# A decode kernel bound by its cache reads: part of the query weights on eight DMA engines, smaller work after the last load

## Chip, cores, metric

One core of one Trainium2 chip. The metric is the device time of one execution in microseconds (us), median over executions.

## The reference

One token (1 x 448) goes through attention with a cache of 65,536 positions for 8 key/value heads of 256, and through a token mixer; a gate mixes the two results.

```python
x = A_x                                             # [1, 1, 448]
g = sigmoid((x * gate_w).sum(-1, keepdims=True))
q = (x @ wq).reshape(1, 1, 16, 256)                 # wq [448, 4096]
p = softmax(q @ k_cache.T / 16)                     # k, v: [1, 8, 65536, 256]
a = (p @ v_cache).reshape(1, 1, 4096) @ wo          # wo [4096, 448]
u = gelu(layernorm(x).T * w1 + b1)
b = (u @ w2 + b2).T
out = g * a + (1 - g) * b
```

Keys and values are 537 MB of the 544 MB that the kernel reads.

## The kernel before

Forty-eight K blocks and as many V blocks (5 or 6 MB each) are loaded in turn into two K buffers and one V buffer. One queue (SP) issues nearly everything. The query weights use the V buffer first. Their first 384 rows lie three to a partition; the other 64 rows are cut in two halves of 2048 columns, which makes 128 rows.

```python
TAIL = 4
...
wqa = vbuf[:, 0:KA * HQ * DH].rearrange("p (k n) -> p k n", k=KA)
wqb = vbuf[:, KA * HQ * DH:KA * HQ * DH + 8 * DH]
do.dma("sp", vbuf[:, 0:KA * HQ * DH], A_wq[0:DA, :].rearrange("(p k) n -> p (k n)", k=KA), writes=["wqa"])
do.dma("sp", wqb, A_wq[DA:D, :].rearrange("r (hh n) -> (r hh) n", hh=2), writes=["wqb"])
...
load_k(0)
load_k(1)
```

The last V block comes in four pieces. The first two go through matmuls with V as the moving operand (`upright`), the last two through small ones with V as the stationary operand (`turned`). `TAIL` is the number of 128-row groups in the last piece. Two pieces of output weights follow.

```python
edges = [0, nlast - TURN - SB, nlast - TURN, nlast - TAIL, nlast]   # 0, 40, 56, 76, 80
...
dve.wait_ge(s_fp, 2)
drain_pv(False).then_inc(s_fd, 1)
dve.tensor_scalar(out=row[:], in0=acc[0:1, 0:D], scalar1=bias[:, 0:1], scalar2=None, op0=ALU.add).then_inc(s_fd, 1)
pe.wait_ge(s_fd, 1)
o_turn(2)
pe.wait_ge(s_last[2], 16)
turned(edges[2], edges[3])
pe.wait_ge(s_last[3], 16)
turned(edges[3], edges[4]).then_inc(s_fp, 1)
dve.wait_ge(s_fp, 3)
heads().then_inc(s_fd, 1)
pe.wait_ge(s_fd, 2)
for a in range(4):                       # bias sums into the output's accumulator
    pe.matmul(acc4[...], lhsT=one_f[:, 0:1], rhs=row[...], start=True, stop=False, ...)
pe.wait_ge(s_fd, 3)
for k in range(4):                       # output projection
    r, cc = divmod(k, 2)
    if cc == 0:
        pe.wait_ge(s_wl[r], 16)
    ...
```

The softmax here doesn't subtract the row's maximum and nothing guards it: scores larger than these inputs give would overflow.

Of the kernel before, what the change touches and what calls it, by code (L numbers as in the profile page):

```python
# [9 lines left out]
BF16 = mybir.dt.bfloat16  # L10
ACT = mybir.ActivationFunctionType
ALU = mybir.AluOpType
# [3 lines left out]
HKV = 8  # L16
# [12 lines left out]


TURN = 24
TAIL = 4

GELU_C0 = 0.7978845608028654
GELU_C1 = 0.044715
# [59 lines left out]
def kernel(  # L95
# [16 lines left out]
    D = A_x.shape[-1]  # L112
# [3 lines left out]
    KA = D // 128  # L116
    DA = KA * 128
    DR = D - DA
    DQ = D // 4
# [7 lines left out]
    const = ctx.enter_context(tc.tile_pool(name="const", bufs=1))  # L127
# [8 lines left out]
    misc = psum.tile([128, 512], FP32, name="misc")  # L136
    den_ps = psum.tile([128, 512], FP32, name="den_ps")
    acc = psum.tile([128, 512], FP32, name="acc")
    acc4 = psum.tile([128, 512], FP32, name="acc4")

    x_row = const.tile([1, D], BF16, name="x_row")
# [10 lines left out]
    one_f = const.tile([1, 128], FP32, name="one_f")  # L152
    col_f = const.tile([128, 1], FP32, name="col_f")
    zero_b = const.tile([1, D], BF16, name="zero_b")
    xd = const.tile([1, 2, 128], BF16, name="xd")
    xw = const.tile([128, KA + 2, 128 + HKV - 1], BF16, name="xw")
    xg = const.tile([1, D], FP32, name="xg")
    gate = const.tile([128, 2], FP32, name="gate")
    half_g = const.tile([128, 1], FP32, name="half_g")
    bias = const.tile([1, 1], FP32, name="bias")  # L160
# [26 lines left out]
    row = const.tile([1, D], FP32, name="row")  # L187
# [19 lines left out]
    def critical():  # L207
        do = Order(nc)
        pe, dve, act, pool, sp = nc.tensor, nc.vector, nc.scalar, nc.gpsimd, nc.sync
# [19 lines left out]

        wqa = vbuf[:, 0:KA * HQ * DH].rearrange("p (k n) -> p k n", k=KA)  # L230
        wqb = vbuf[:, KA * HQ * DH:KA * HQ * DH + 8 * DH]
        do.dma(
            "sp", vbuf[:, 0:KA * HQ * DH], A_wq[0:DA, :].rearrange("(p k) n -> p (k n)", k=KA),
            writes=["wqa"],
        )
        do.dma("sp", wqb, A_wq[DA:D, :].rearrange("r (hh n) -> (r hh) n", hh=2), writes=["wqb"])

        def load_k(i):
            n = steps[i] * SB * DH
# [24 lines left out]
        for k, src in enumerate((B_w1[0, :], B_b1, B_w2[:, 0])):  # L264
# [7 lines left out]
                out=ident[:], in_=ident[:], compare_op=ALU.not_equal, fill=1.0, base=0,  # L272
# [23 lines left out]
        for hh in range(2):  # L296
            do(
                "dve", lambda e: e.tensor_copy(
                    out=xd[:, hh, :].rearrange("o (r two) -> o r two", two=2)[:, :, hh],
                    in_=x_row[:, DA:D],  # L300
                ), reads=["x_row"], writes=["xd"],
            )
        x_ps = misc[:, 480:480 + KA + 2]

        def turn_x(e):
            for k in range(KA + 2):
                if k < KA:
                    src = x_row[:, 0:DA].rearrange("o (p k) -> o p k", k=KA)[:, :, k]
                else:
                    src = xd[:, k - KA, :]  # L310
                last = e.matmul(
                    x_ps[:, k:k + 1], lhsT=src, rhs=one_b[0:1, 0:1], start=(k == 0),
                    stop=(k == KA + 1), skip_group_check=True,
                )
            return last

# [1 line left out]
        do(  # L318
            "dve", lambda e: e.tensor_copy(
                out=xw[:, :, HKV - 1:HKV + 96:32],  # L320
                in_=x_ps.rearrange("p (k o) -> p k o", o=1).to_broadcast([128, KA + 2, 4]),
            ), reads=["x_ps"], writes=["xw"],
        )

# [3 lines left out]
            reads=["x_row", "gw_row"], writes=["xg"],  # L328
# [3 lines left out]
            reads=["xg"], writes=["zb"],  # L332
# [3 lines left out]
            writes=["zb1"],  # L336
# [4 lines left out]
            reads=["one_f", "zb", "zb1"], writes=["z_ps"],  # L341
        )
        for col, sign in ((0, -1.0), (1, 1.0)):
            do(
                "act", lambda e: e.activation(
                    out=gate[:, col:col + 1], in_=z_ps[:, 0:1], func=ACT.Exp, scale=sign
# [5 lines left out]
                out=gate[:], in0=gate[:], scalar1=1.0, scalar2=None, op0=ALU.add  # L352
# [5 lines left out]
                out=half_g[:], in0=gate[:, 1:2], scalar1=0.5, scalar2=None, op0=ALU.mult  # L358
# [4 lines left out]
                out=bias[:], in0=z_ps[0:1, 1:2], in1=gate[0:1, 1:2], op=ALU.mult  # L363
# [6 lines left out]
            reads=["one_b", "x_row"], writes=["xb_ps"],  # L370
# [5 lines left out]
                out=veps[:], in0=mv[:, 1:2], scalar1=1e-5, scalar2=None, op0=ALU.add  # L376
# [4 lines left out]
            reads=["veps", "mhalf"], writes=["rstd"],  # L381
        )
        for _ in range(2):
            do(
                "dve", lambda e: e.tensor_tensor(out=nt[:], in0=rstd[:], in1=rstd[:], op=ALU.mult),
                reads=["rstd"], writes=["nt"],
# [3 lines left out]
                reads=["nt", "veps"], writes=["nt"],  # L390
# [3 lines left out]
                    out=nt[:], in0=nt[:], scalar1=-0.5, scalar2=1.5, op0=ALU.mult, op1=ALU.add  # L394
# [4 lines left out]
                reads=["rstd", "nt"], writes=["rstd"],  # L399
# [3 lines left out]
                out=h_bc[:], in0=xb_ps, scalar1=mv[:, 0:1], scalar2=rstd[:, 0:1],  # L403
                op0=ALU.subtract, op1=ALU.mult,
# [17 lines left out]
        for k, (t, key) in enumerate(((w1T, "w1T"), (b1T, "b1T"))):  # L422
            do(
                "dve", lambda e: e.tensor_copy(out=t[:], in_=w_ps[:, k * NF:(k + 1) * NF]),
                reads=["w_ps"], writes=[key],
# [3 lines left out]
                out=hw2[:], in0=w_ps[:, 2 * NF:3 * NF], scalar1=half_g[:, 0:1], scalar2=None,  # L429
                op0=ALU.mult,  # L430
# [6 lines left out]
                out=mask[:].rearrange("p m x -> p (m x)"), in_=pat[:].rearrange("p m x -> p (m x)")  # L437
# [4 lines left out]
        q_ps = sc  # L442

        def project(e):
            for n in range(HKV):
                half, at = divmod(n, 4)
                for k in range(KA + 1):
                    if k < KA:
                        rhs = wqa[:, k, n * 512:(n + 1) * 512]
                    else:  # L450
                        k, rhs = KA + half, wqb[:, at * 512:(at + 1) * 512]
                    last = e.matmul(
                        q_ps[:], lhsT=xw[:, k, HKV - 1 - n:HKV - 1 - n + 128], rhs=rhs,
                        start=(n == 0 and k == 0), stop=(n == HKV - 1 and k >= KA),
                        skip_group_check=True,
                    )
            return last

        do("pe", project, reads=["wqa", "wqb", "xw"], writes=["q_ps"])
        do.need("sp", writes=["wqa", "wqb"])  # L460
        load_v(0)
        load_wo(0)
        do(
# [1 line left out]
                out=q_row[:].rearrange("p (m c y) -> p m y c", c=2, y=32),  # L465
                in_=q_ps[:].rearrange("p (m y c) -> p m y c", c=2, y=32),
# [4 lines left out]
                out=qr[:].rearrange("p r q n -> p (r q n)"), in_=q_row[:]  # L471
# [11 lines left out]
        for r in range(2):  # L483
# [4 lines left out]
                skip_group_check=True,  # L488
# [21 lines left out]
        for r in range(2):  # L510
            at = (HKV - 1) * 512 + r * DH
            sp.dma_start(
                out=wo[:, r, :, :].rearrange("p c n -> p (c n)"),
                in_=A_wo[at:at + DH, :].rearrange("(p c) n -> p (c n)", c=2),
# [52 lines left out]
        with nc.Fori(0, HKV, 1, engines=[DVE], head_slot={DVE: 128}) as turn_v:  # L567
            for c in range(PER):
# [21 lines left out]
                else:  # L590
# [6 lines left out]
                        out=og[:], in0=og[:], scalar1=dsum[:, 0:1], scalar2=None, op0=ALU.add  # L597
# [8 lines left out]
        for i in range(total):  # L606
            g, c = divmod(i, PER)
            ins = act.activation(  # L608
                out=p_t[:], in_=sc[:], func=ACT.Exp, scale=scale, accum_out=den[:, c:c + 1]
# [3 lines left out]
            b, ph = divmod(i - 2, 2)  # L613
            if not 0 <= b < NF:
                continue
            if ph == 0:
                ins = act.activation(  # L617
                    out=t_b[:], in_=h_bc[:], func=ACT.Square, scale=w1T[:, b:b + 1],
                    bias=b1T[:, b:b + 1],
# [9 lines left out]
        for b in range(NF):  # L629
            work = [  # L630
                lambda: pool.tensor_scalar(  # L631
                    out=u_b[:], in0=h_bc[:], scalar1=w1T[:, b:b + 1], scalar2=b1T[:, b:b + 1],
                    op0=ALU.mult, op1=ALU.add,
# [48 lines left out]
        def o_turn(width):  # L682
            for half, m in enumerate((L0, H0)):
                for cc in range(2):
                    ins = pe.matmul(  # L685
                        o_ps[:, cc, 0:width if half == 0 else 2],
                        lhsT=og[:, half * DH + cc:(half + 1) * DH:2],
                        rhs=mask[:, m:m + (width if half == 0 else 2), 0],
                        start=(half == 0 and cc == 0), stop=(half == 1 and cc == 1),
                        skip_group_check=True,  # L690
                    )
            return ins
# [54 lines left out]
        def turned(lo, hi):  # L747
# [10 lines left out]
        pe.wait_ge(s_mp, 6 * NF)  # L758
        pe.matmul(
            acc[0:1, 0:D], lhsT=col_f[:], rhs=ymix[:], start=False, stop=True, skip_group_check=True,  # L760
        )
        take(pe, s_pt)
        pe.wait_ge(s_last[0], 16)
        upright(edges[0], edges[1])
# [2 lines left out]
            den_ps[:, 0:2], lhsT=dsum[:].to_broadcast([128, 128]), rhs=mask[:, D0:D0 + 2, 0],  # L767
            start=True, stop=True,
        ).then_inc(s_fp, 1)
        dve.wait_ge(s_fp, 1)  # L770
        rden_gate(den_ps[:, 0:2])
        pe.wait_ge(s_last[1], 16)
        upright(edges[1], edges[2]).then_inc(s_fp, 1)
        dve.wait_ge(s_fp, 2)
        drain_pv(False).then_inc(s_fd, 1)
        dve.tensor_scalar(
            out=row[:], in0=acc[0:1, 0:D], scalar1=bias[:, 0:1], scalar2=None, op0=ALU.add
        ).then_inc(s_fd, 1)
        pe.wait_ge(s_fd, 1)
        o_turn(2)  # L780
        pe.wait_ge(s_last[2], 16)
        turned(edges[2], edges[3])
        pe.wait_ge(s_last[3], 16)
        turned(edges[3], edges[4]).then_inc(s_fp, 1)
        dve.wait_ge(s_fp, 3)
        heads().then_inc(s_fd, 1)
        pe.wait_ge(s_fd, 2)
        for a in range(4):
            pe.matmul(  # L789
                acc4[32 * a:32 * a + 1, 0:DQ], lhsT=one_f[:, 0:1], rhs=row[:, DQ * a:DQ * (a + 1)],  # L790
                start=True, stop=False, tile_position=(0, 32 * a), skip_group_check=True,
            )
        pe.wait_ge(s_fd, 3)
        for k in range(4):
            r, cc = divmod(k, 2)
# [6 lines left out]
                    tile_position=(0, 32 * a), skip_group_check=True,  # L802
                )
        ins.then_inc(s_fp, 1)
        dve.wait_ge(s_fp, 4)
        dve.tensor_copy(out=res[0:97, :], in_=acc4[0:97, 0:DQ]).then_inc(s_fd, 1)  # L806
        s_out = nc.alloc_semaphore("s_out")
        sp.wait_ge(s_fd, 4)
# [37 lines left out]
```

## Time and profile before

| | before |
|---|---|
| median of 3 runs | 1265.99 us (1265.82 to 1266.15) |
| span of the profiled run | 1264.1 us |
| DMA queue 1 | 99.7% of sixteen engines' time |
| last V piece lands, last of sixteen engines | 1259.20 us |
| last output weights land | 1260.41 us |
| output projection ends | 1261.01 us |

The DMA engines are the bound: queue 1 takes 99.7% of their time, and no compute engine is busy for over 57%. What decides tenths of a microsecond is when the latest of the sixteen engines lands its last bytes, and how much work follows. Both are read from the chain of waits and from the trace's record of semaphore increments, sixteen for each full load. An engine ends its share of a load with a closing record, a packet of 4 bytes; the increment that the waiting engine sees follows it (in the last query-weight load: closing records from 11.14 to 12.21 us, increments from 11.46 to 12.52, 0.30 to 0.37 us later, paired in order of time). A load has landed at its last increment. "Narrow load" below means the load that runs on eight engines alone, "low" are those eight and "high" the other eight. The end of the projection is the end of its last matmul's record (1261.01); the chain puts it at 1261.04. The prediction below shows the lines.

### The profile page before, as it was taken

The page shows a single profiled execution, that of the slowest core. Times are in us where ns is not written, and L with a number is a line of the kernel's source. Part 1 is how long each engine was busy: PE and PEld are TensorE (multiplying, and loading weights), DVE is VectorE, ACT ScalarE, POOL GpSimd, SP SyncE. Part 2 cuts the span into 40 slices and gives each one's busy share as a digit, 9 for nine tenths or more (in the row PEclk, how much of TensorE's full clock was granted, in tenths as well). Part 3 has the DMA queues.
Part 4 walks back from the last instruction along what each step waited for, and adds up shares of the span by engine and source line. Part 5 has one row for each costly group of instructions (what it writes and reads, how often), then busy time and mean ns, then how long its engine had stood idle before and what let it go on. Part 6 is the DMA issues. An engine that isn't in the chain of part 4 may idle for free. (4 is left out here: it accounts for less than half of the span.)

```text
span 1264.1 us, 10623 instructions
## 1 busy us (share of the span) xinstructions
PE 722.2 (57%) x4296; PEld 276.3 (22%) x4296; DVE 675.3 (53%) x462; ACT 50.1 (4%) x127; POOL 78.5 (6%) x111
## 2 busy tenths in 40 slices
PE   3855656456554665556654564555645656466556
PEld 1311222122221222112221221222212222122212
DVE  5745554465544555455555555464545645465544
ACT  0000000000000000000000000000000000000000
POOL 1001010110110101101011011000000000000000
PEclk9887777878787787777878787777877778778887
DMA  9999999999999999999999999999999999999998
GB/s 407 425 435 429 442 435 424 439 433 432 440 430 426 436 434 437 440 426 434 438 427 438 430 436 436 430 432 436 430 443 429 429 439 434 429 442 430 430 436 348
DMA packets 16840, 544.30 MB, mean 431 GB/s; under 512 B 1856, under 2 KB 3906, under 8 KB 4162
## 3 DMA queue, kind: packets, MB, share of 16 engines
q1 hardware_dynamic: 16744, 544.22, 99.7%
q8 instruction: 2, 0.03, 0.0%
q10 hardware_dynamic: 90, 0.01, 0.0%
q14 instruction: 4, 0.03, 0.0%
HBM read 544.22 MB, written 0.00 MB: 431 GB/s over the span
## 5 line engine op out<-in xcount | busy, mean ns | idle before, releaser
L661 PE MATMUL sc<-kT,qw 128*128 128x512 bf16 x2048 | 573.5, 438 | 482.9 <-PEq L657 482.9
L532 DVE STREAM_TRANSPOSE kT<-kbuf 128x2048 f32<-128x2048 f32 x256 | 572.8, 2285 | 330.1 <-DVEq L524 330.1
L661 PEld LDWEIGHTS sc<-kT,qw 128*128 128x128 bf16 x2048 | 211.1, 108 | 845.1 <-issue 692.8
L675 PE MATMUL pv<-vbuf,pT 128*4 128x512 bf16 x2008 | 121.2, 390 | 28.8 <-PEq L705 28.7
L543 DVE TENSOR_TENSOR og<-pv,og 128x512 f32<-128x512 f32 x40 | 27.7, 692 | 98.5 <-DVEq L524 97.9
L608 ACT ACTIVATE p_t<-sc 128x512 bf16<-128x512 f32 x48 | 28.7, 597 | 1191.9 <-PE sc L661 1191.9
L675 PEld LDWEIGHTS pv<-vbuf,pT 128*4 128x4 bf16 x2008 | 47.1, 88 | 99.3 <-issue 53.8
L589 DVE STREAM_TRANSPOSE pT<-p_t 128x512 bf16<-128x512 bf16 x32 | 22.8, 712 | 74.1 <-DVEq L524 74.1
L635 POOL TENSOR_SCALAR t_b<-t_b 128x448 f32<-128x448 f32 x14 | 7.9, 564 | 359.1 <-ACT t_b L617 359.1
L639 POOL TENSOR_SCALAR t_b<-t_b,hw 128x448 f32<-128x448 f32 x14 | 8.9, 638 | 334.0 <-ACT t_b L625 334.0
L579 DVE STREAM_TRANSPOSE pT<-p_t 128x512 bf16<-128x512 bf16 x8 | 5.7, 712 | 26.9 <-DVEq L524 26.9
L720 PE MATMUL acc<-wo,oT 128*1 128x448 bf16 x28 | 10.1, 504 | 12.7 <-PEq L717 12.7
L644 POOL TENSOR_TENSOR ymix<-ymix,t_b 128x448 f32<-128x448 f32 x14 | 16.1, 1148 | 1.1
L638 POOL TENSOR_TENSOR t_b<-t_b,u_b 128x448 f32<-128x448 f32 x14 | 15.8, 1127 | 1.2
L643 POOL TENSOR_TENSOR t_b<-t_b,u_b 128x448 f32<-128x448 f32 x14 | 15.8, 1126 | 1.2
L542 DVE COPY og<-pv 128x512 f32<-128x512 f32 x8 | 5.5, 692 | 18.9 <-DVEq L524 18.9
L594 DVE STREAM_TRANSPOSE pT<-p_t 128x512 bf16<-128x512 bf16 x8 | 5.7, 712 | 14.9 <-DVEq L524 14.9
L617 ACT ACTIVATE t_b<-h_bc,b1T,w1T 128x448 f32<-128x448 f32 x14 | 10.5, 748 | 0.0
L631 POOL TENSOR_SCALAR u_b<-h_bc,w1T,b1T 128x448 f32<-128x448 f32 x14 | 10.0, 715 | 4.1 <-DVE hw L428 2.7
L608 ACT ACTIVATION_READ_ACCUMULATOR p_t<-sc 128x1 f32 x48 | 9.3, 194 | 0.0
L685 PEld LDWEIGHTS misc<-mask,og 128*128 128x128 f32 x64 | 8.7, 196 | 2.4 <-DVE og L543 1.3
L477 DVE TENSOR_TENSOR qw<-qr,block 128x32 bf16<-128x32 f32 (+1 forms) x18 | 8.6, 561 | 0.1
(86 smaller groups left out, 77.4 us busy)
## 6 DMA issues: line engine op xcount, KB each, us to landing
kbuf<-in_A_k_cache_dram SPq DMA_DIRECT2D x32, 5120.0 KB, 33.2
vbuf<-in_A_v_cache_dram SPq DMA_DIRECT2D x31, 5120.0 KB, 20.4
kbuf<-in_A_k_cache_dram SPq DMA_DIRECT2D x16, 6144.0 KB, 35.7
vbuf<-in_A_v_cache_dram SPq DMA_DIRECT2D x16, 6144.0 KB, 23.5
wo<-in_A_wo_dram SPq DMA_DIRECT2D x7, 448.0 KB, 23.6
vbuf<-in_A_wq_dram SPq DMA_DIRECT2D x1, 3072.0 KB, 10.3
kbuf<-in_A_v_cache_dram SPq DMA_DIRECT2D x1, 2560.0 KB, 26.0
kbuf<-in_A_v_cache_dram SPq DMA_DIRECT2D x1, 1280.0 KB, 30.5
```

The costliest lines, as they stand in the source:

```text
L532: dve.transpose(out=kT[b][:].bitcast(FP32), in_=kn[:, s * SB * 128:(s + 1) * SB * 128]).then_inc(s_kt, 1)
L543: return dve.tensor_tensor(out=og[:], in0=pv[:], in1=og[:], op=ALU.add)
L589: dve.transpose(out=pT[:], in_=p_t[:]).then_inc(s_pt, 1)
L608: ins = act.activation(out=p_t[:], in_=sc[:], func=ACT.Exp, scale=scale, accum_out=den[:, c:c + 1])
L617: ins = act.activation(out=t_b[:], in_=h_bc[:], func=ACT.Square, scale=w1T[:, b:b + 1], bias=b1T[:, b:b + 1],)
L631: lambda: pool.tensor_scalar(out=u_b[:], in0=h_bc[:], scalar1=w1T[:, b:b + 1], scalar2=b1T[:, b:b + 1], op0=ALU.mult, op1=ALU.add,),
L638: lambda: pool.tensor_tensor(out=t_b[:], in0=t_b[:], in1=u_b[:], op=ALU.mult),
L643: lambda: pool.tensor_tensor(out=t_b[:], in0=t_b[:], in1=u_b[:], op=ALU.mult),
L644: lambda: pool.tensor_tensor(out=ymix[:], in0=ymix[:], in1=t_b[:], op=ALU.add),
L661: ins = pe.matmul(sc[:], lhsT=qw[:, q, at:at + 128], rhs=kv[:, :, q // 2, :, q % 2], start=(first and q == 0), stop=(last and q == 7), ski ...
L675: ins = pe.matmul(pv[32 * a:32 * a + 4, :], lhsT=pT[:, k, :, ROW0 + s], rhs=vt[:, j * DH:(j + 2) * DH], start=first and k < 4, stop=last a ...
L720: ins = pe.matmul(acc[0:1, 0:D], lhsT=oT[:, k:k + 1], rhs=wo[:, r, cc, :], start=False, stop=False, skip_group_check=True,)
```

## The change

The intent is to take a little load off eight DMA engines, to leave less work behind the last load, and to have the bias sums done early.

```diff
-TAIL = 4
+TAIL = 10
...
-        do.dma("sp", wqb, A_wq[DA:D, :].rearrange("r (hh n) -> (r hh) n", hh=2), writes=["wqb"])
+        rows = A_wq[DA:D, :].rearrange("r (hh n) -> (r hh) n", hh=2)
+        do.dma("sp", wqb[:, 512:2048], rows[:, 512:2048], writes=["wqb"])
+        do.dma(
+            "sp", wqb[:, 0:512], rows[:, 0:512].rearrange("(b a) n -> a b n", a=8), writes=["wqc"],
+        )
...   # two more columns of x, in the permuted row order, for the matmuls with these 512 columns
+            do(
+                "dve", lambda e: e.tensor_copy(
+                    out=xd[:, 2 + hh, :].rearrange("o (q two b) -> o q two b", two=2, b=16)[:, :, hh],
+                    in_=x_row[:, DA:D].rearrange("o (b q) -> o q b", q=4),
+                ), reads=["x_row"], writes=["xd"],
+            )
...   # after the matmul that adds ymix to acc
+        dve.wait_ge(s_fp, 1)
+        dve.tensor_scalar(out=row[:], in0=acc[0:1, 0:D], scalar1=bias[:, 0:1], ...).then_inc(s_fd, 1)
...   # the row operation after drain_pv and the four bias matmuls after turned() are gone from there
         pe.wait_ge(s_fd, 1)
+        for a in range(4):
+            pe.matmul(acc4[...], lhsT=one_f[:, 0:1], rhs=row[...], start=True, stop=False, ...)
+        pe.wait_ge(s_fd, 2)
         o_turn(2)
```

More of the change, by code (lines that the diff above doesn't have):

```diff
@@ L154 @@
     zero_b = const.tile([1, D], BF16, name="zero_b")
-    xd = const.tile([1, 2, 128], BF16, name="xd")
-    xw = const.tile([128, KA + 2, 128 + HKV - 1], BF16, name="xw")
+    xd = const.tile([1, 4, 128], BF16, name="xd")
+    xw = const.tile([128, KA + 4, 128 + HKV - 1], BF16, name="xw")
     xg = const.tile([1, D], FP32, name="xg")
@@ L302, in critical @@
             )
-        x_ps = misc[:, 480:480 + KA + 2]
+            do(
[4 more added lines that the diff above has]
+            )
+        x_ps = misc[:, 480:480 + KA + 4]
         def turn_x(e):
-            for k in range(KA + 2):
+            for k in range(KA + 4):
                 if k < KA:
@@ L312, in turn_x @@
                     x_ps[:, k:k + 1], lhsT=src, rhs=one_b[0:1, 0:1], start=(k == 0),
-                    stop=(k == KA + 1), skip_group_check=True,
+                    stop=(k == KA + 3), skip_group_check=True,
                 )
@@ L320, in critical @@
                 out=xw[:, :, HKV - 1:HKV + 96:32],
-                in_=x_ps.rearrange("p (k o) -> p k o", o=1).to_broadcast([128, KA + 2, 4]),
+                in_=x_ps.rearrange("p (k o) -> p k o", o=1).to_broadcast([128, KA + 4, 4]),
             ), reads=["x_ps"], writes=["xw"],
@@ L450, in project @@
                     else:
-                        k, rhs = KA + half, wqb[:, at * 512:(at + 1) * 512]
+                        k = KA + half + (0 if at else 2)
+                        rhs = wqb[:, at * 512:(at + 1) * 512]
                     last = e.matmul(
@@ L457, in project @@
             return last
-        do("pe", project, reads=["wqa", "wqb", "xw"], writes=["q_ps"])
-        do.need("sp", writes=["wqa", "wqb"])
+        do("pe", project, reads=["wqa", "wqb", "wqc", "xw"], writes=["q_ps"])
+        do.need("sp", writes=["wqa", "wqb", "wqc"])
         load_v(0)
@@ L760, in critical @@
             acc[0:1, 0:D], lhsT=col_f[:], rhs=ymix[:], start=False, stop=True, skip_group_check=True,
-        )
+        ).then_inc(s_fp, 1)
+        dve.wait_ge(s_fp, 1)
+        dve.tensor_scalar(
+            out=row[:], in0=acc[0:1, 0:D], scalar1=bias[:, 0:1], scalar2=None, op0=ALU.add
+        ).then_inc(s_fd, 1)
         take(pe, s_pt)
@@ L769, in critical @@
         ).then_inc(s_fp, 1)
-        dve.wait_ge(s_fp, 1)
+        dve.wait_ge(s_fp, 2)
         rden_gate(den_ps[:, 0:2])
@@ L773, in critical @@
         upright(edges[1], edges[2]).then_inc(s_fp, 1)
-        dve.wait_ge(s_fp, 2)
+        dve.wait_ge(s_fp, 3)
         drain_pv(False).then_inc(s_fd, 1)
-        dve.tensor_scalar(
-            out=row[:], in0=acc[0:1, 0:D], scalar1=bias[:, 0:1], scalar2=None, op0=ALU.add
-        ).then_inc(s_fd, 1)
         pe.wait_ge(s_fd, 1)
+        for a in range(4):
+            pe.matmul(
+                acc4[32 * a:32 * a + 1, 0:DQ], lhsT=one_f[:, 0:1], rhs=row[:, DQ * a:DQ * (a + 1)],
+                start=True, stop=False, tile_position=(0, 32 * a), skip_group_check=True,
+            )
+        pe.wait_ge(s_fd, 2)
         o_turn(2)
@@ L784, in critical @@
         turned(edges[3], edges[4]).then_inc(s_fp, 1)
-        dve.wait_ge(s_fp, 3)
+        dve.wait_ge(s_fp, 4)
         heads().then_inc(s_fd, 1)
-        pe.wait_ge(s_fd, 2)
-        for a in range(4):
-            pe.matmul(
-                acc4[32 * a:32 * a + 1, 0:DQ], lhsT=one_f[:, 0:1], rhs=row[:, DQ * a:DQ * (a + 1)],
-                start=True, stop=False, tile_position=(0, 32 * a), skip_group_check=True,
-            )
         pe.wait_ge(s_fd, 3)
@@ L804, in critical @@
         ins.then_inc(s_fp, 1)
-        dve.wait_ge(s_fp, 4)
+        dve.wait_ge(s_fp, 5)
         dve.tensor_copy(out=res[0:97, :], in_=acc4[0:97, 0:DQ]).then_inc(s_fd, 1)
```

## The prediction

> **What bounds the kernel now.** I read the page's head and slices, its queue table, the chain that ended last, then the timelines of both ends.
>
> ```profile
> span 1264.1 us, 10623 instructions
> PE 722.2 (57%) x4296; PEld 276.3 (22%) x4296; DVE 675.3 (53%) x462; ACT 50.1 (4%) x127; POOL 78.5 (6%) x111
> DMA  9999999999999999999999999999999999999998
> q1 hardware_dynamic: 16744, 544.22, 99.7%
> ```
>
> No compute engine is busy for over 57%, while the sixteen DMA engines are busy in every slice and queue 1 fills 99.7% of their time. The bound is moving 544 MB. The windows view gives 434 GB/s between 40 and 1225 us, and that stretch is not touched by the change. What is left are the two ends, in tenths of a microsecond.
>
> ```profile
> 1228.07 30.50 DMA kbuf<-in_A_v_cache_dram
> 1258.57 0.05 issue
> 1258.62 1.44 PE misc L751 x48
> 1260.06 0.48 PE acc L789 x8
> 1260.54 0.50 PE acc L799 x16
> ```
>
> This is the chain in order of time (start, duration). The third of four pieces of the last V block lands at 1258.57; 48 small matmuls (30 ns each) follow; then the bias matmuls (L789), the output projection (L799), a copy and the store. L799 really waits for the vector engine, as the timeline says:
>
> ```profile
> 1256.22 0.69 DVE L543 TENSOR_TENSOR og<-pv,og 128x512 f32<-128x512 f32 x1 [0.59 <-PE pv L740]
> 1256.83 0.66 DVE L776 TENSOR_SCALAR row<-acc,bias 1x448 f32<-1x448 f32 x1
> 1256.97 1.10 PE L685 MATMUL misc<-mask,og 128*128 128x2 f32 x8 [0.80 <-DVE og L543]
> 1260.09 0.16 DVE L550 TENSOR_TENSOR oT<-misc,rden 128x4 bf16<-128x4 f32 x1 [2.60 <-PE misc L751]
> 1260.46 0.28 PEld L799 LDWEIGHTS acc<-wo,oT 128*1 128x1 bf16 x16 [0.38 <-DVE oT L550]
> ```
>
> The trace also records each DMA engine's increment of a load's semaphore. The last of sixteen for the four V pieces and the two output-weight pieces came at 1253.08, 1255.52, 1258.57, 1259.20, 1260.00 and 1260.41. In the K and V loads of the stream the sixteen engines keep nearly fixed distances, since each works through its own queue without a gap: around 70 us they stand 0 to 0.93 us behind the first, and one stands 1.73 us behind. That one, call it L, is 0.80 us later than the next and sets every landing. It fell back at one event: an instruction packet of 16,384 bytes at 29.52 us (1.109 us) on its chain of packets; its next data semaphore came 1.60 us late. A second such packet (1257.98, 0.98 us) holds up another engine, F, which had been about 0.6 us behind the first; so F and L are the last two of the final output-weight piece (1260.37, 1260.41).
>
> [...] the 14-row loads show one early and 14 later increments, the one-row loads one and one. [...]
>
> **The change, part by part.**
>
> *Query weights.* The remainder block was one load of 128 rows of 4096 bytes, 8 rows to an engine. Now 3072 bytes of each row go over 16 engines and the last 1024 in a load whose source has an outer dimension of 8[...]: sixteen rows for each low engine, none for the high ones. Packets followed each other every 912 ns at 24,576 bytes and 155.5 ns at 4096. That is 0.0369 ns per byte plus 4.2 ns; so 117.7 ns at 3072 and 42.0 at 1024. Before: 8 x 155.5 = 1244 ns per engine. After, low: 8 x 117.7 + 16 x 42.0 = 1614 (+0.37 us). High: 942 (-0.30 us). As the queues never run dry, this offset should last to the end. It helps if L is among the high eight and hurts if it is low. If L is high, the next engine (0.80 ahead of L) can at most come to 0.80 - 0.67 = 0.13 ahead, so L's whole 0.30 us counts.
>
> *Its cost at the start.* Two more tiny matmuls, two copies (0.21 us each), larger memsets (about 0.25 us) before 4.74 us: the vector engine then waits until 6.76 for another load, so nothing. The projection began at 13.02, behind the bias chain (its own weights had landed at 12.52); a low engine's later share would land near 12.9. One more issue on SP (0.41 us) lies behind queued data. The V load that waits for the projection at 21.74 has the K loads, landing up to 42.4, ahead of it. All hidden.
>
> *TAIL from 4 to 10.* The third piece falls from 20 to 14 row blocks of 512 bytes (10,240 to 7168 bytes per partition), the fourth grows from 4 to 10. By the formula the third takes 8 x 269 = 2.15 us after 1255.52, so 1257.67 (the old size by the same formula gives 3.06, measured 3.05). The fourth takes 1.55, so 1259.22, as before. PE: L685 ends at 1258.07; 28 matmuls, 0.84 us, to 1258.91; from 1259.27 the last 20, 0.60 us, to 1259.87. Before 1260.06: a gain of 0.19 us.
>
> *Bias sums earlier.* The 0.66 us row operation moves to the vector engine's gap near 1254.7. It delays the reciprocal from 1255.08 to about 1255.35, done by 1255.9, before the drain at 1256.22. The four bias matmuls (0.55 us) run beside the 0.69 us drain. They leave the path after L751, but L799 starts 0.40 us after L751 anyway, for the vector engine. Worth 0 to 0.05 us.
>
> *What stops the gain.* L799's second half needs the last output weights, landed at 1260.41; with 0.27 us of matmuls its floor is about 1260.75, and it ended at 1261.04. So without better landings no more than 0.29 us is to be had; 0.19 fits below it.
>
> **Rivals and the sum.** (A) L and F both high: V 0.30 earlier, turned matmuls end at 1259.57, output weights at 1260.11: -0.5 us. (B) L high, F low: the output weights land at 1260.78 through F, the second half of L799 ends near 1261.09: about 0. (C) L low: last piece at 1259.59, matmuls to 1260.24: +0.2 us. For L high speaks only that someone chose the low eight for the extra bytes, presumably having seen which lag. Against: L stood in the middle at the start (sixth of sixteen), which says nothing[...]. I take 0.65 for high, and a half for F: 0.33 x -0.5 + 0.32 x 0 + 0.35 x 0.2 = -0.1. (D) The longer program moves the instruction fetch to another engine or time: L's 1.60 us delay would strike an engine with another offset, from -0.2 to +0.7 us. (E) The narrow load delays the projection so far that the stream runs dry: it would need 20 us, and I don't believe it.
>
> **Range and chances.** From 1265.99, between A and the mean, since such a change was probably made on a measurement: 1265.8 us. A plus scatter (the three runs span 0.33 us) sets the low end, 1265.2; C with D the upper, 1266.5. 2% would be 25 us, and no part of the change reaches a twentieth of that: same 0.98, faster 0.01, slower 0.01.
>
> **What would show it.** Right: 544 MB at an unchanged rate between 40 and 1225 us; the narrow load with eight late increments of its semaphore; the distance of the latest engine from the next in the stream falling from 0.80 to about 0.13 (A, B), or growing to about 0.80 or 1.5 (C); L751 split into 28 and 20; L789 ahead of L685. Wrong: a stream with gaps, another engine as laggard, or a last half of L799 that waits for output weights.

The sum: 0.33 x -0.5 + 0.32 x 0 + 0.35 x 0.2 = -0.1 us; its 0.65 was the author's estimate. That the load with an outer dimension of 8 would run on eight engines was the author's assumption when this was written. The run after shows it: one early and eight later increments (12.23 to 12.99 us) and 128 packets of 1024 bytes. The trace gives no engine numbers. "Without a gap" is what the packets of queue 1 before show: they fall into sixteen chains, and of 15,072 packets between 40 and 1225 us all but three start within 5 ns of the end of the packet ahead (those three 302 or 303 ns after it). The formula, 0.0369 ns per byte plus 4.2 ns, is an estimate from the two spacings that stand beside it.

## More of the kernel before

All runs here are of the fast state.

An engine's K excess is what its first packet of the first K block takes over 1.815 us.

## The result

| | before | after |
|---|---|---|
| median of 6 runs | 1265.99 us | 1265.86 us |
| lowest to highest | 1265.80 to 1266.15 | 1265.70 to 1266.01 |
| span of the profiled run | 1264.1 | 1263.9 |
| last V piece lands | 1259.20 | 1259.26 |
| last output weights land | 1260.41 | 1260.44 |
| output projection ends | 1261.01 | 1260.84 |

The ratio is 0.9999, 95% interval 0.9986 to 1.0012. (A ratio is the mean time of one kernel's fast runs over that of the other's of the same rounds, so not quite the ratio of the medians quoted.) By the clock this is "the same". The trace resolves more.

The head of the page after, its DMA slices, its queue row and its row for the long middle stretch of the windows view (busy time and count of each engine, granted clock, DMA share, GB/s):

```profile
span 1263.9 us, 10631 instructions
DMA  9999999999999999999999999999999999999998
q1 hardware_dynamic: 16880, 544.22, 99.7%
40.00:1225.00 1185.00, 678.42 (x4012) 258.94 (x4015) 634.42 (x401) 47.18 (x120) 73.73 (x83) 0.79 1.00 434
```

The same row of the kernel before:

```profile
40.00:1225.00 1185.00, 680.08 (x4008) 258.87 (x4010) 634.42 (x401) 47.16 (x120) 73.73 (x83) 0.79 1.00 434
```

Nothing moved in the middle: 434 GB/s in both. The chain that ended last, in order of time (start, duration, what):

```profile
1228.49 30.77 DMA kbuf<-in_A_v_cache_dram
1259.26 0.05 issue
1259.30 0.71 PE misc L763 x20
1260.01 0.02 issue
1260.04 0.17 DVE oT L562
1260.21 0.04 issue
1260.25 0.61 PE acc L812 x16
```

It now starts from the fourth piece, issued at 1228.49, and only 20 turned matmuls follow its landing. The bias matmuls are gone from it. The timeline shows them earlier, with the row operation that feeds them:

```profile
1254.38 0.67 DVE L775 TENSOR_SCALAR row<-acc,bias 1x448 f32<-1x448 f32 x1
1256.16 0.37 PE L794 MATMUL acc<-row,one_f 1*1 1x112 f32 x8
1256.29 0.69 DVE L555 TENSOR_TENSOR og<-pv,og 128x512 f32<-128x512 f32 x1 [0.71 <-PE pv L752]
1257.03 1.10 PE L697 MATMUL misc<-mask,og 128*128 128x2 f32 x8 [0.50 <-DVE og L555]
```

So the tail is shorter, as planned. But the last V piece lands no earlier (1259.26 against 1259.20). The weights were to bring it 0.30 us forward, if the latest engine was among the high eight. The trace's packet records say what happened. These are the first K packets of the sixteen engines, 49,152 bytes each, the first that follow the query weights (start and duration in ns, read from the packed trace):

```
before  11147+1815 11285+1815 11352+1815 11365+1815 ... 12156+1815 12215+1815   (all sixteen 1815)
after   11021+2154 11043+2158 11198+2154 11203+2151 11347+2145 11357+2136 11442+2135 11510+2151
        11640+2102 11720+2114 11771+2080 11887+2075 11927+2069 11998+2066 12215+1973 12233+1973
```

The engine L of the prediction is recognised by the 16,384-byte instruction packet in its chain. Its packets follow each other every 1812 ns, so the chain can be followed back. After the change L starts K at 11,043 ns, before any engine that carries narrow packets can (the narrow load's closing records come from 11.63 us on; eight engines start K before that). So L is one of the high eight. It starts K 0.35 us earlier than before (11,391 ns), and its first K packet takes 0.34 us longer. It ends that packet at 13,201 ns against 13,206: nothing is left. One pair of profiles could mislead, since L's start scatters by 0.15 us between kernels of the same loads. The means say the same: in four profiles without a narrow load L ends this packet at 13.21 to 13.36 us (mean 13.30), in three with the change's narrow load at 13.20, 13.25 and 13.33 (mean 13.26), and the last V piece lands at 1259.30 in the mean of both groups.

### The profile page after: what moved, and what is told of

It is laid out like the page before. It is cut to its first block, busy times and chain, and to the rows that moved or that the text cites. A ratio compares the mean times of both kernels' runs of the same rounds, so it can differ in the third digit from the quotient of the medians.

```text
span 1263.9 us, 10631 instructions
## 1 busy us (share of the span) xinstructions
PE 720.0 (57%) x4298; PEld 276.2 (22%) x4298; DVE 676.4 (54%) x464; ACT 50.1 (4%) x127; POOL 78.4 (6%) x111
## 3 DMA queue, kind: packets, MB, share of 16 engines
q1 hardware_dynamic: 16880, 544.22, 99.7%
```

## The experiments

First the parts apart. In each section the times are the median of the run and of the kernel before in the same rounds.

**w_only**: the weights part alone.

```diff
-TAIL = 10
+TAIL = 4
# and the tail code of the kernel before
```

> The query-weights part alone (piece size 4 and the old place of the bias sums kept). If the narrow load gives back what it saves (my theory after the first look: the first K packet of every engine took 1.97 to 2.16 us in place of 1.815), the last V piece lands within 0.1 us of before (1259.20), the first K packets are again over 1.95 us, and the median stays within 0.15 us of before. If instead the change's 0.2 us comes from the weights, the last V piece lands 0.2 to 0.3 us earlier.

Measured: 1265.97 us against 1265.92. The first K packets took 1.95 to 2.11 us, the last V piece landed at 1259.32. The weights alone give nothing. (One of its four times was 1268.59. Single high times came in other runs too: 1266.66 in tail10_oldbias, 1266.86 in high64, 1267.70 in after_again. None was profiled, and nothing is built on them.)

**t_only**: the two tail parts alone.

```diff
-TAIL = 4
+TAIL = 10
# and the early bias sums; query weights as before
```

> Piece size 10 and the early bias sums alone, weights as before. If these make the whole gain: third and fourth V pieces land near 1257.6 and 1259.2, turned matmuls end near 1260.0, the span is 0.15 to 0.25 us under before, and all first K packets take 1.815 us. If the weights make the gain, the span is as before within 0.1 us.

Measured: 1265.79 us against 1265.92. All first K packets took 1.815 us. The third and fourth pieces landed at 1257.80 and 1259.37, both 0.2 us later than expected, and the turned matmuls ended at 1260.12: L happened to end its first K packet 0.11 us later than in the kernel before, and its instruction packet took 1.165 us in place of 1.109. The span was 1264.0, so the expected 0.15 to 0.25 us under before was not met as a span. From the landing of the last V piece to the end of the projection it took 1.55 us, against 1.80 in the kernel before and 1.78 in w_only: the tail's gain is 0.23 to 0.25 us, and a landing that differs by 0.17 us between loads of the same form hides much of it.

**tail10_oldbias**: the new piece size alone.

> The kernel before with piece size 10 alone, bias sums in their old place. If the early bias sums are worth nothing, the output projection starts about 0.37 us after the last turned matmul ends, and the distance from the last V landing to the end of the projection equals that with both parts (1.59 us), within 0.06 us. If they count, it is longer by 0.1 us or more.

```diff
-TAIL = 4
+TAIL = 10
# everything else as before
```

Measured: 1265.86 us against 1265.88. From the last V landing (1259.36) to the projection's end it took 1.675 us. So the piece size is worth 1.803 - 1.675 = 0.13 us and the bias sums 1.675 - 1.554 = 0.12 us, from one profile each; kernels with both parts and the same loads at the end lie between 1.48 and 1.62 us. To the start of the projection, which the landing of the last output weights can't hold back, the bias sums save 1.134 - 0.987 = 0.15 us. Its chain shows what they cost:

```profile
1259.36 0.05 issue
1259.41 0.68 PE misc L751 x20
1260.09 0.48 PE acc L789 x8
1260.57 0.50 PE acc L799 x15
```

The bias matmuls (L789) stand between the turned matmuls and the projection on the tensor engine. Its timeline has the vector engine's result (oT) ready at 1260.29 and the projection's first matmul at 1260.50, 0.21 us later; in the changed kernel, without bias matmuls there, it is 0.05 us (1260.20 to 1260.25). So the bias matmuls, not the vector engine, held the projection back.

Then the long K packets.

**split16**: both shares over all sixteen engines, in natural row order.

```diff
-            "sp", wqb[:, 0:512], rows[:, 0:512].rearrange("(b a) n -> a b n", a=8), writes=["wqc"],
+            "sp", wqb[:, 0:512], rows[:, 0:512], writes=["wqc"],
# x in natural order for these columns
```

> The changed kernel with the 1024-byte share loaded in natural row order over all sixteen engines (same two packet sizes, no narrow load). If the long first K packets come from two packet sizes or from the small packets as such, they stay near 2.1 us. If they come from low engines writing to partitions that other engines are filling, they fall to about 1.815 us, and the mean position of the engines at the end of the first K load is 0.2 us or more earlier than in the changed kernel.

Measured: 1265.89 us against 1265.92. All sixteen first K packets are back at 1.815 us. The increments at the end of the first K load come on average at 26.47 us, against 26.84 in the changed kernel and 26.40 in the kernel before. So neither the small packets nor the two sizes are the cause. What is left is the narrow load, or its row order, which this run changes too; own32 and own32_high below have equal row orders and tell them apart.

**low64**: the narrow load written to partitions 0 to 63 only.

```diff
-            "sp", wqb[:, 0:512], rows[:, 0:512].rearrange("(b a) n -> a b n", a=8), writes=["wqc"],
+        part = A_wq[DA:D, :].rearrange("r (hh n) -> r hh n", hh=2)[:, :, 0:512]
+        for hh in range(2):      # wqc: 64 partitions, two halves of 512 columns
+            do.dma("sp", wqc[:, hh, :], part[:, hh, :].rearrange("(b a) n -> a b n", a=8), ...)
# one x column for 64 partitions in that order; these matmuls contract over 64 partitions
```

> The changed kernel with the same 128 KB on the same eight engines and the same source rows, but written to partitions 0 to 63 only (two loads of 64 rows by 1024 bytes). Theory (contention at the destination): the eight high engines' first K packets are back at 1.815 us, the latest engine keeps its saving, and the last V piece lands 0.2 to 0.35 us earlier than in the changed kernel (1259.26). Rival (contention at the source or in the memory): the high engines' first K packets are still over 1.95 us and the landing does not move by more than 0.1 us.

Measured: 1265.92 us against 1265.92. The first K packets took 1.90 to 2.03 us: less, not gone, and the first seven engines to start K, too early to have carried narrow packets, were still at 1.98 to 2.01. The excess over 1.815 us, summed over the engines, is 2.55 us against 4.60 in the changed kernel (3.85 in w_only). The last V piece landed at 1259.21. My expectation failed as put; the rival fits as well. Which partitions the high engines fill is not shown, so the theory doesn't say why bytes for partitions 0 to 63 slow them. The next two runs separate them.

**high64**: the same to partitions 64 to 127.

```diff
-        wqc = vbuf[0:64, ...]
+        wqc = vbuf[64:128, ...]
# x for partitions 64 to 127 likewise
```

> As the run with partitions 0 to 63, but written to partitions 64 to 127[...]. Theory (contention at the destination): the slowing of the high engines' first K packets doubles, 0.3 to 0.6 us over 1.815 against 0.2 with partitions 0 to 63, and the last V piece lands 0.2 us or more later than there (1259.21). Rival (source or memory): the same first K packets as with partitions 0 to 63, within 0.1 us.

Measured: 1266.03 us against 1265.88. The first K packets took 1.98 to 2.35 us, the sum of the excess is 6.56 us, and the last V piece landed at 1259.41. The loads are those of low64 but for the destination, which alone raises the excess from 2.55 to 6.56 us. The destination counts. On the engines that start K first the excess went from 0.20 to 0.49 us, so it more than doubled.

**own32**: four loads of 32 rows in place of two of 64.

```diff
-        for hh in range(2):
-            do.dma("sp", wqc[:, hh, :], part[:, hh, :].rearrange("(b a) n -> a b n", a=8), ...)
+        for hh in range(2):
+            for j in range(2):
+                do.dma(
+                    "sp", wqc[32 * j:32 * j + 32, hh, :],
+                    part[32 * j:32 * j + 32, hh, :].rearrange("(b a) n -> a b n", a=8), ...
+                )
# x in that order; the rest as low64
```

The thought was that fewer engines would then meet at the same partitions. It was a guess: no run here shows which engine wrote which partition.

> The changed kernel with the same 128 KB on the same eight engines, written in four loads of 32 rows each (partitions 0 to 31 and 32 to 63)[...]. Theory (several narrow-load engines meet at the same partitions, or meet another engine's data there): [...]the first K packets are back at 1.815 us on all engines, the narrow load's increments come about 0.34 us after its last packets in place of 0.6 to 0.8, and the latest engine gains: last V piece at 1258.9 to 1259.1. Rival (the source order of the rows, or the memory): first K packets still over 1.9 us, no gain.

Measured: 1265.39 us (1265.33 to 1265.65) against 1265.88. All first K packets took 1.815 us. The eight increments of the last of the four loads came 0.33 to 0.51 us after the engines' closing records, in place of 0.59 to 0.89 us for the changed kernel's narrow load (closing records from 11.63 to 12.23, increments from 12.22 to 12.99, paired in order of time). L ends its first K packet at 13.02 us, against 13.20 to 13.33 in the other kernels with a narrow load to low or all partitions. The last V piece landed at 1258.98. Its chain:

```profile
1258.98 0.05 issue
1259.03 0.69 PE misc L772 x20
1259.72 0.03 issue
1259.75 0.17 DVE oT L571
1259.92 0.04 issue
1259.96 0.62 PE acc L821 x16
```

**own32_high**: the control, the same four loads to partitions 64 to 127.

```diff
-        wqc = vbuf[0:64, ...]
+        wqc = vbuf[64:128, ...]
```

> A control: the four-load version with the same loads, rows and engines, and only the destination moved from partitions 0 to 63 to partitions 64 to 127. If the destination decides, the first K packets are again well over 1.815 us (2.0 us or more on the engines that start K first) and the gain is gone: last V piece at 1259.2 to 1259.5, median 1265.8 to 1266.1. If the four-load form or its row order decides, it is as good as the four-load version: 1.815 us, 1258.9 to 1259.1.

Measured: 1265.98 us against 1265.83. First K packets 2.03 to 2.56 us, last V piece at 1259.52. With loads and rows the same, the destination alone takes the gain away and more: 0.54 us between the landings.

**own32_again** and **after_again**, on one chip.

> The four-load version again, five rounds, for a surer time: 1265.3 to 1265.6 us, 0.3 us or more under the kernel before of the same rounds and every run below its median. The last V piece lands at 1258.9 to 1259.1. If the first time was luck of the start, it comes back to 1265.7 to 1265.9.

> The changed kernel itself beside it on the same chip: 0.1 to 0.2 us under the kernel before (from the two tail parts), first K packets again 1.95 us or more, and 0.3 us or more above the four-load version.

Measured: the kernel before 1265.83 us. The changed kernel 1265.75, first K packets 1.95 to 2.16 us, last V piece at 1259.34. The four-load version had two times of 1265.26 and 1265.32 and three of 1266.24 to 1266.40, median 1266.24. Its profiled execution is one of the early ones (span 1263.5, last V piece at 1258.93). My expectation of the time failed, and with it the 0.3 us that the changed kernel was to lie above it.

**own32_look1** and **own32_look2**: the same kernel, in search of a profile of the later group.

> The four-load version fell into two groups of times, six runs at 1265.3 to 1265.65 and three at 1266.2 to 1266.4. This looks for a profile of the later group. If one of the instruction fetches strikes a later engine in it, the latest engine of the stream stands about 1 us further behind the mean than the 0.64 us of the early group; if the loads start later, all engines stand later. If the profile falls in the early group again (span 1263.5), the cause stays open.

> The same again, a second chance of a profile of the later group, and six more times: if the groups belong to the chip or the session, the times of these two runs agree with each other; if they are drawn anew in each execution, about a third lie at 1266.2 to 1266.4.

Measured, the kernel before at 1265.95 us: look1 gave 1265.42 to 1265.52, all four early; look2 gave 1265.56 and then 1266.25, 1266.44 and 1266.48, on the same chip. So the groups do not go with the chip. Both profiled executions are early ones (last V piece at 1259.01 and 1259.02), so no profile of the later group exists.

All seventeen times of the four-load version: eleven from 1265.26 to 1265.65, six from 1266.24 to 1266.48. The changed kernel has two groups too (1265.70 to 1265.72 and 1266.00 to 1266.01 in the first six runs), and split16 (1265.67, 1265.69 and 1266.09, 1266.24) and low64 (1265.59, 1265.70 and 1266.15, 1266.23). In its early group the four-load version is faster than every run of the kernel before of the same rounds; in the later it is slower than all.

### The readings together

Times in us from the traces. The K excess is the sum over the sixteen engines of what the first K packet takes over 1.815.

| kernel | narrow load to | K excess | L ends first K packet | last V piece lands | output weights land | projection ends |
|---|---|---|---|---|---|---|
| before | none | 0 | 13.21 | 1259.20 | 1260.41 | 1261.01 |
| t_only | none | 0 | 13.31 | 1259.37 | 1260.53 | 1260.93 |
| tail10_oldbias | none | 0 | 13.36 | 1259.36 | 1260.51 | 1261.04 |
| split16 | none | 0 | 13.33 | 1259.25 | 1260.38 | 1260.79 |
| after | 0 to 127 | 4.60 | 13.20 | 1259.26 | 1260.44 | 1260.84 |
| after_again | 0 to 127 | 3.80 | 13.25 | 1259.34 | 1260.50 | 1260.81 |
| w_only | 0 to 127 | 3.85 | 13.33 | 1259.32 | 1260.49 | 1261.10 |
| low64 | 0 to 63 | 2.55 | 13.20 | 1259.21 | 1260.38 | 1260.78 |
| high64 | 64 to 127 | 6.56 | 13.47 | 1259.41 | 1260.63 | 1261.03 |
| own32_high | 64 to 127, by 32 | 7.04 | 13.49 | 1259.52 | 1260.70 | 1261.10 |
| own32 | 0 to 63, by 32 | 0 | 13.02 | 1258.98 | 1260.16 | 1260.56 |
| own32_again | 0 to 63, by 32 | 0 | 13.01 | 1258.93 | 1260.10 | 1260.50 |

## Why the prediction was right or wrong

The time and the range were right, the time in part by luck: 1265.8 was set between case A and the mean of all cases, and the saving that A rests on was lost. What gain there was came from the tail. The range, 1265.2 to 1266.5, holds "no change" too, so it tests no step. Two steps failed, in what follows: that L's saving lasts, and what the bias sums are worth.

*The bound, the middle, the start.* Right. The projection began at 13.12 us in place of 13.02, because the narrow load's last increment came at 12.99, not 12.9; nothing waited for it later.

*L is among the high eight (0.65).* Right: it carries no narrow packets.

*"As the queues never run dry, this offset should last to the end" and "L's whole 0.30 us counts".* This step failed, and it is the main one. The saving was there at the start of K (0.35 us) and was lost in the first K packet (0.34 us). The arithmetic gave each engine only its own packets. The narrow load's bytes also held up the packets of engines that carry none of them (L's first K packet took 2.158 us in place of 1.815), depending on where they are written (K excess 6.56 us in high64 against 2.55 in low64, 7.04 in own32_high against 0 in own32: only the destination differs). Cases A, B and C each presupposed that this offset lasts, so none of them happened. Where the destination does no harm the step is right in size: the last V piece landed at 1258.93 to 1259.02 in four profiles of the four-load version, mean 1258.99, and at 1259.20 to 1259.37 in the four kernels without a narrow load, mean 1259.30. That is 0.31 us, against the 0.30 worked out. The forecast sign, a distance of 0.13 us from L to the next engine, came out as 0.035 us, but not because L had moved up: a low engine, struck by the other instruction fetch of that time (8192 bytes), closed the second K load at 42.04 us, 1.06 us later than the engine so struck before. L closed it at 42.01, 0.02 us later than before. So another engine stood level with L, which the prediction had named as a sign of being wrong.

*TAIL.* The landings were right (1257.67 and 1259.22 predicted, 1257.70 and 1259.26 measured). The last 20 matmuls were mis-sized, 0.60 us against 0.71 to their end, so the part gave 0.13 us and not 0.19.

*Bias sums, "worth 0 to 0.05 us".* The step that failed is "L799 starts 0.40 us after L751 anyway, for the vector engine". That wait was for the bias matmuls ahead on the tensor engine; the chain of waits had said so (0.48 us of L789), and I preferred the timeline's named releaser. Measured: 0.12 us at the end of the projection and 0.15 at its start. With the bias matmuls gone, the projection starts 0.21 us after the vector operation starts (1260.04 to 1260.25) in place of 0.37.

*What stops the gain.* The limit is real, and after the change it binds; the prediction had named a last half that waits for output weights as a sign of being wrong. (By the 0.34 us from landing to end that it assumed, its case B would end at 1261.12 and not 1261.09; nothing hangs on this.) The sixteen projection matmuls wait in two halves of eight. Their starts in the trace, in ns, with the landing of the last output weights:

```
after   first half 1260252 to 1260311   weights landed 1260437   second half from 1260480
own32   first half 1259965 to 1260024   weights landed 1260159   second half from 1260202
```

In both the second half starts 43 ns after the weights and ends 0.40 us after them (0.34 assumed); so it does in t_only, low64, high64 and own32_high, and after_again starts it 43 ns after too, but ends 0.31 after. Before it was 0.59 us. The profile's chain names the vector engine alone ahead of L812. So the tail parts took 0.19 us from the time after the last weights; with this order of the matmuls no more was to be had there.

*Rivals.* D, another engine struck by the instruction fetch, didn't happen in any profile that I followed: L was a high engine in the changed kernel, w_only, low64 and after_again (the smaller fetch, of 8192 bytes, did strike a low one: in the changed kernel that engine starts K at 11.72 us, after its closing record of the narrow load at 11.71). But the two groups of times remain. If in some executions the fetch strikes a low engine, the narrow load should, by the forecast's estimate, cost it 0.37 us where it saves a high one 0.30, so the gap between the groups should be 0.67 us wider in the four-load version. Its group means are 1265.43 and 1266.34, a gap of 0.9 us; in split16, without a narrow load, the gap is 0.5. That is the right sign and somewhat small. But other kernels with such a load on the low engines don't bear it out: the gap is 0.3 in the changed kernel's first six runs and 0.55 in low64. So it is not shown, and no later execution was profiled. Why the early and late groups exist stays open, and so does why low64 left an excess of 2.55 us on all engines. Shown is that the destination decides; the mechanism is not.

## What to carry to other kernels

In this kernel, whose DMA queue fills 99.7% of the engines' time, the delay that one instruction packet of 16,384 bytes gave the latest engine (1.60 us) lasted: L stood 1.79 us behind the first engine at 42 us and 1.69 at the last V piece. Giving such an engine less to carry moved the landing of the last V piece forward by 0.31 us in four early profiles, but only where the bytes taken off it were written without slowing the others (own32 against own32_high: 0.54 us between the landings, with the destination alone changed). So count where bytes are written as well as which engine carries them. Check such a shift by the first packets that follow it and not by the time alone: every verdict here is "the same". Work that was placed on an engine just ahead of a waiting instruction may be the wait (0.48 us of L789 here). Neither the named releaser nor the chain is enough by itself: the first missed L789, the second missed the output weights.
